# Opening of an attention and soft-MoE kernel: a load on another queue, two operations on another engine, and banks of two pools

## The chip, the cores and the metric

One core of one Trainium2 chip runs the kernel. The metric is the device time of one execution in microseconds (us). The kernel before took 471.74 us, the median of three runs (471.3 to 471.97).

## The reference

Two stages follow each other. The first is an attention over B = 4 batches and H = 8 heads (32 heads in all), with S = 768 rows of D = 64 columns, in which a query sees a key only if the two fall in the same bucket of a hash of six signs:

```python
q_bits = (np.einsum('bhsd,dk->bhsk', q, proj) > 0)
k_bits = (np.einsum('bhsd,dk->bhsk', k, proj) > 0)
mask = q_bucket[:, :, :, None] == k_bucket[:, :, None, :]
scores = scale * np.matmul(q, k.transpose(0, 1, 3, 2))
scores = np.where(mask, scores, -1000000000.0)
scores = scores - np.max(scores, axis=-1, keepdims=True)
attn = np.exp(scores)
attn = attn / (np.sum(attn, axis=-1, keepdims=True) + 1e-09)
return np.matmul(attn, v)
```

The second is a soft mixture of eight experts on the 3072 rows of 512 columns that the first leaves: softmaxes over the rows and over the 32 slots, and two matrix products per expert. The change lies in the first 10 us of the first stage.

## The kernel before

Everything is in float32 (or its rounded form for the matmuls), transposed so that the 64 columns of a head lie on partitions. Two heads share a tile. The 32 heads run one after the other, overlapped; the order of the work is written by hand: every step is a small function that `at` puts into `plan` with a due time from the tables ONCE (first occurrences) and STEADY (the rest). `plan` is sorted by these times and the functions are called in that order, so on each engine and each queue the order of instructions is the order of the due times. Those of the opening are negative, from -120 on.

A head needs two tiles, `Y` and `X`, which the scores multiply in two passes. `Y` holds the high part of q and of k (rows 0 to 63), the hash bits as rows of signs (from row 64) and, sent later, the negated maxima of the rows; `X` holds cross terms. Head 0 gets its parts by a short path written for the opening, the other heads by copies.

The steps around the change, in the order of the due times:
- Loads: `first` (projection and constants, line 278), then the four halves of q and k of heads 0 and 1 (`load_half`, line 257, L259), then head 2's q and k (`load`, L255) and v, all on SP's queue.
- `spin` (line 320, L323): matmuls on a tile of ones, whose results nobody reads; 7 at the start, 1 after nearly every matmul of head 0's maxima, 2 at three later places.
- `first_copy` (L429, ScalarE), `first_bits` (line 431, L435, PE): the hash projections of head 0 for k (x = 1) and q (x = 0), into two banks of pool `p_st`.
- `more_bits` (line 442): the projections of heads 0 and 1 from the full tiles (L411), copied by ScalarE (L447) into `pts[0]`; `bits_rest` (line 449) turns them into signs on GpSimd (L406 there) for head 1, tile `bt`.
- `first_over` (line 424, L406 on VectorE): the same for head 0, in five pieces, from PSUM straight into `Y`.
- `first_hi` (L440, ScalarE) the high parts; `split_lo` (L375, GpSimd) the low parts; `copy_ident` (L337, GpSimd) the identity for transposes.
- `smax` (line 463): the scores of a block of 128 rows for the maxima alone, a matmul (L474) and the maximum on VectorE (L477, L480). A bank takes 512 columns of them, so that a head has nine maxima; the banks are the two of pool `p_sm`.
- `shift`, `shift_rows` (L489 to L502): the maxima are joined, transposed on PE (L499), copied by ScalarE (L502) and sent as `mr` into a row of `Y` by SP.
- Copies between partitions by DMA (`move`, L379): `spread_y`, `spread_bits` (four copies of `bt`, head 1) and `spread_l`, `spread_x` for the later heads on SP's queue; for head 0 `spread_l` and `spread_x` go on ScalarE's queue. `first_x` (L403, ScalarE) fills the rest of head 0's `X`.
- `scores` (L515, PE): the true scores, followed by the exponential on ScalarE (L519), the sums on GpSimd (L526, L532) and the product with v (L544).

PSUM has eight banks here: two of `p_sm`, three of `p_st`, one of `p_av` (spins and the product with v) and two of `p_mi`.

Of the kernel before, what the change touches and what calls it, by code (L numbers as in the profile page):

```python
# [9 lines left out]
F32 = mybir.dt.float32  # L10
# [80 lines left out]
    ('copy_ident',): -79.0, ('first_bits', 0): -117.0, ('first_bits', 1): -119.0, ('first_copy', 0): -116.0,  # L91
    ('first_copy', 1): -118.0, ('first_hi', 0): -107.0, ('first_hi', 1): -108.0, ('first_mz',): -96.0,
    ('first_over', 0, 0, 256): -110.0, ('first_over', 0, 256, 512): -100.0, ('first_over', 0, 512, 768): -99.0,
    ('first_over', 1, 0, 512): -111.0, ('first_over', 1, 512, 768): -109.0, ('first_rows', 0): -115.0,
# [95 lines left out]
def lsh_attention_soft_moe(  # L190
# [66 lines left out]
    def load_half(a):  # L257
        for x in (1, 0):
            nc.sync.dma_start(out=raw[D * a:D * a + D, x], in_=qk[x, 0, D * a:D * a + D])  # L259

# [4 lines left out]


    ones = cp.tile([P, 32], F32, name="ones")
    nc.vector.memset(ones, 1.0)
    XYs = [held.tile([P, 2, 2, S], F32R, name=f"XY{i}") for i, held in enumerate((yp, xp, yq))]
    Xs, Ys = [[t[:, :, n] for t in XYs] for n in range(2)]  # L270
    idle = Xs[2][:, 0, 0:P + 512]
    nc.vector.memset(idle.bitcast(F32), 1.0)
    eps = cp.tile([P, 1], F32, name="eps")
# [45 lines left out]

    def spin(n, cols=512):  # L320
        pt = p_av.tile([P, 512], F32, name="av")
        for _ in range(n):
            nc.tensor.matmul(pt[:, 0:cols], idle[:, 0:P], idle[:, P:P + cols], start=True, stop=True)  # L323

    spin(7)


# [77 lines left out]
    def over(out, pt, rows, eng=nc.vector, cols=slice(0, HC)):  # L405
        eng.tensor_scalar(out=out, in0=pt[rows, cols], scalar1=con[rows, C_TH:C_TH + 1],  # L406
                          scalar2=con[rows, C_AM:C_AM + 1], op0=ALU.is_gt, op1=ALU.mult)
# [16 lines left out]
    def first_over(x, a, b):  # L424
        j = 2 * x + a // 512
        over(Ys[0][64:80, x, a:b], first_pt[x], slice(32 * j, 32 * j + 16), cols=slice(a % 512, a % 512 + b - a))

# [35 lines left out]
    def smax(h, t, part):  # L463
        s = st[h]
        if "mx" not in s:
            s["mx"] = mp.tile([P, NT, 2], F32, name="mx", bufs=2)
        mx = s["mx"].rearrange("p t a -> p (t a)")
        n = 2 * t + part
        key = "sm", n // 4, (n % 4 + 1) // 2
        if key not in s:  # L470
            s[key] = p_sm.tile([P, 512], F32, name="smx")
        pt = s[key]
        o, a, b = ((0, 0, 512), (0, 512, S), (256, 0, 256), (0, 256, S))[n % 4]
        nc.tensor.matmul(pt[:, o:o + b - a], Ys[h % N_Y][0:96, 0, t * P:(t + 1) * P], Ys[h % N_Y][0:96, 1, a:b],  # L474
                         start=True, stop=True)
        if n % 4 == 2:
            nc.vector.tensor_reduce(out=mx[:, n - 1:n + 1], in_=pt.rearrange("p (a x) -> p a x", a=2),  # L477
                                    axis=AX.X, op=ALU.max)
        elif n % 4 != 1:
            nc.vector.reduce_max(out=mx[:, n:n + 1], in_=pt, axis=AX.X)  # L480
        if h == 0 and t < NT - 1:
            spin(1)

# [381 lines left out]
    for n in (1, 0):  # L865
        at(first_copy, n)
        at(first_bits, n)
        at(first_hi, n)
    for xab in ((1, 0, 512), (0, 0, 256), (1, 512, S), (0, 256, 512), (0, 512, S)):
        at(first_over, *xab)  # L870
    at(more_bits)
    for n in range(3):
        at(spin, 2, tag=n)
    at(bits_rest)
# [264 lines left out]
```

## Time and profile before

| | |
|---|---|
| median of three runs | 471.74 us |
| the profiled execution | 471.47 us |
| its span, first to last instruction | 469.7 us |
| PE busy | 456.4 us (97%) |
| VectorE, ScalarE, GpSimd busy | 389.0, 247.4, 327.6 us |
| first DMA issue on SP | at 0.74 us |
| ScalarE's table load (L298) | at 0.74 us, 1.28 us long |

Times in the views are in us from the first instruction. PE is TensorE's matmuls, PEld its weight loads, DVE is VectorE, ACT ScalarE, POOL GpSimd. A queue's own instructions are those of SPq and ACTq: issuing a DMA takes the queue some time, and the data starts later. L with a number is the line of the kernel; since `over` and `move` are helpers, several steps share the lines L406 and L379, and are told apart by the tiles (`XY<-bt`, `XY<-stage`, `XY<-mr`).

### The profile page before, as it was taken

Reading aid. Unit: us, or ns where it says so; the run is one execution under the profiler, and the core shown is the slowest. Engines: PE = TensorE matmul, PEld = TensorE weight load, DVE = VectorE, ACT = ScalarE, POOL = GpSimd, SP = SyncE. Lnnn points to the kernel's source line nnn. Section 1 sums busy time; section 2 is a strip of 40 time slices with the busy share of each in tenths; the row PEclk is TensorE's granted clock in tenths of the full one; section 3 lists DMA queues with packets and bytes.
Section 4 is the critical chain, followed back from the end, with each engine's and each line's share of the span. In section 5 each row is a group of like instructions: output and inputs, shape, how many; then the busy total and the mean of one; then the engine's idle time right before and its main releaser. Section 6 shows DMA issues by size and latency. Waiting matters only on the chain.

```text
span 469.7 us, 10655 instructions
## 1 busy us (share of the span) xinstructions
PE 456.4 (97%) x3980; PEld 287.8 (61%) x3980; DVE 389.0 (83%) x723; ACT 247.4 (53%) x462; POOL 327.6 (70%) x205
## 2 busy tenths in 40 slices
PE   7999999999999999999999999999999999999993
PEld 3565666666666666666656666666666666553472
DVE  7868898989798988889898989897979886787952
ACT  5364556464657555555556464646565545531242
POOL 7878778878775988787868987787759878810000
PEclk9999999999999999999999999999999999999998
DMA  5757677777774767878683878685846677899997
GB/s 159 200 139 165 162 170 230 163 238 164 218 172 150 170 194 165 238 167 241 145 235 106 205 203 202 206 202 159 200 135 166 177 180 258 297 387 409 408 365 305
DMA packets 39535, 99.29 MB, mean 211 GB/s; under 512 B 7326, under 2 KB 13612, under 8 KB 39484
## 3 DMA queue, kind: packets, MB, share of 16 engines
q1 hardware_dynamic: 39292, 98.16, 72.3%
q8 instruction: 31, 0.51, 0.4%
q10 hardware_dynamic: 160, 0.39, 0.4%
q14 instruction: 20, 0.16, 0.1%
q0 software_dynamic: 32, 0.07, 0.0%
HBM read 52.76 MB, written 6.29 MB: 126 GB/s over the span
## 4 chain that ended last, share of the span: by engine, by line
PE 91%; DVE 3%; DMA 2%; issue 1%; ACT 0%; SPq 0%; DVEq 0%; ACTq 0%
PE st L515 29%; PE av L544 25%; PE smx L474 16%; PE qs L1050 3%; PE qh L1000 3%; PE mi L556 2%; PE mi L411 2%; PE mi L607 2%; PE mi L572 2%; DMA XY<-mr 1%; PE mi L592 1%; DMA stage<-qk 1%; PE mi L762 1%; PE mi L499 1%; PE qh L1070 1%
## 5 line engine op out<-in xcount | busy, mean ns | idle before, releaser
L532 POOL TENSOR_TENSOR acc<-acc,pt 128x768 f32<-128x768 f32 x125 | 229.1, 1833 | 9.6
L519 ACT ACTIVATE pt<-st 128x512 f32<-128x512 f32 x288 | 164.3, 597 | 62.3 <-PE st L515 56.5
L515 PE MATMUL st<-XY 128*128 128x256 f32 (+1 forms) x768 | 178.0, 347 | 0.7 <-DMA XY<-mr 0.7
L480 DVE TENSOR_REDUCE mx<-smx 128x1 f32<-128x512 f32 x192 | 131.1, 688 | 24.9 <-PE smx L474 22.8
L515 PEld LDWEIGHTS st<-XY 128*128 128x128 f32 x768 | 125.0, 189 | 19.0 <-ACT pt L519 1.7
L544 PE MATMUL av<-pt,v 128*32 128x384 f32 x1536 | 133.1, 486 | 0.0
L474 PE MATMUL smx<-XY 96*128 96x512 f32 (+1 forms) x384 | 118.4, 357 | 1.2 <-DVE mx L477 0.9
L526 POOL TENSOR_TENSOR acc<-pt 128x768 f32<-128x768 f32 x32 | 58.9, 1839 | 53.1 <-ACT pt L519 53.1
L544 PEld LDWEIGHTS av<-pt,v 128*32 128x32 f32 x1536 | 49.7, 110 | 72.8 <-issue 71.6
L474 PEld LDWEIGHTS smx<-XY 96*128 96x128 f32 x384 | 66.0, 188 | 30.8 <-issue 9.6
L477 DVE TENSOR_REDUCE mx<-smx 128x2 f32<-128x512 f32 x96 | 65.8, 686 | 6.1 <-PE smx L474 5.5
L548 ACT COPY avs<-av 128x384 f32<-128x384 f32 x32 | 15.3, 477 | 82.9 <-PE av L544 82.8
L564 DVE RECIPROCAL dl<-sm 128x128 f32<-128x128 f32 x45 | 38.8, 915 | 13.9 <-ACT sm L559 10.1
L372 DVE TENSOR_REDUCE stage<-stage 128x768 fp32r<-128x1536 f32 x28 | 49.0, 1782 | 0.0
L365 ACT ACTIVATE stage<-stage 128x768 fp32r<-128x768 f32 x28 | 22.6, 836 | 5.3 <-DMA stage<-qk 3.8
L609 DVE TENSOR_TENSOR xq<-mi,r 128x256 f32<-128x256 f32 x45 | 17.4, 416 | 1.1 <-PE mi L607 1.1
L833 DVE STREAM_TRANSPOSE w<-call 32x256 f32<-32x256 f32 (+2 forms) x48 | 14.9, 333 | 1.7 <-PE qh L1000 1.1
L1050 PE MATMUL qs<-w 128*32 128x128 f32 (+1 forms) x352 | 15.3, 303 | 0.0
L607 PE MATMUL mi<-ident,avs 128*128 128x128 f32 x90 | 14.8, 272 | 0.0
L607 PEld LDWEIGHTS mi<-ident,avs 128*128 128x128 f32 x90 | 11.7, 140 | 4.0
L1050 PEld LDWEIGHTS qs<-w 128*32 128x32 f32 x352 | 10.6, 110 | 5.2 <-issue 2.2
L411 PE MATMUL mi<-stage,pb 128*32 128x384 f32 x120 | 12.8, 498 | 0.7 <-DMA stage<-qk 0.7
(183 smaller groups left out, 330.8 us busy)
## 6 DMA issues: line engine op xcount, KB each, us to landing
w<-w SPq DMA_DIRECT2D x53, 512.0 KB
XY<-stage SPq DMA_DIRECT2D x62, 384.0 KB
XY<-stage SPq DMA_DIRECT2D x62, 192.0 KB
stage<-qk SPq DMA_DIRECT2D x28, 384.0 KB
v<-vt SPq DMA_DIRECT2D x32, 192.0 KB
out<-stage SPq DMA_DIRECT2D x12, 512.0 KB
stage<-w SPq DMA_DIRECT2D x7, 512.0 KB
xq<-w SPq DMA_DIRECT2D x3, 512.0 KB
```

Source lines behind the costliest of these rows:

```text
L372: nc.vector.tensor_reduce(out=w[:, 2 * x + 1], in_=stage[:, x:n + 1:n - x].rearrange("p t s -> p s t"), axis=AX.X, op=ALU.add, negate=True)
L474: nc.tensor.matmul(pt[:, o:o + b - a], Ys[h % N_Y][0:96, 0, t * P:(t + 1) * P], Ys[h % N_Y][0:96, 1, a:b], start=True, stop=True)
L477: nc.vector.tensor_reduce(out=mx[:, n - 1:n + 1], in_=pt.rearrange("p (a x) -> p a x", a=2), axis=AX.X, op=ALU.max)
L480: nc.vector.reduce_max(out=mx[:, n:n + 1], in_=pt, axis=AX.X)
L515: nc.tensor.matmul(pt[:, o:o + b - a], x[:, 1, i * P:(i + 1) * P], x[:, 0, a:b], start=first, stop=not first)
L519: nc.scalar.activation(pts[i // 2][:, 512 * u:512 * u + 512], pt, AF.Exp, scale=D ** -0.5)
L526: nc.gpsimd.tensor_tensor(out=s["acc"], in0=pr[:, 0:S], in1=pr[:, S:2 * S], op=ALU.add)
L532: eng.tensor_tensor(out=s["acc"], in0=s["acc"], in1=pr[:, a * S:(a + 1) * S], op=ALU.add)
L544: nc.tensor.matmul(s["av"][D * c + d:D * c + d + 32, 0:HC], s["v"][:, i, d:d + 32], pr[:, o + c * HC:o + (c + 1) * HC], start=(i == 0), st ...
L564: nc.vector.reciprocal(out=st[h]["rs"][:, k * P:(k + 1) * P], in_=st[h]["sm"][:, k * P:(k + 1) * P])
L607: nc.tensor.transpose(pt[:, o:o + P], st[h + a]["avs"][:, k * P:(k + 1) * P], ident)
L1050: nc.tensor.matmul(po[32 * j:32 * j + 32], hTs[g][:, f, 32 * j:32 * j + 32], wt[1, x, 2 * g + f // 4, j].rearrange("p (f m) -> p f m", f=4 ...
```

## The change

One half of k goes on ScalarE's queue. The spins take 256 columns instead of 512 and are doubled in number, and the tile of ones that they read is smaller and is filled first. The pieces of `first_over` of q from column 256 on go to GpSimd, with due times before `bits_rest`; since they are read there from `pts[0]`, a new step `first_out` copies them out of PSUM on ScalarE. Of head 0's maxima every second bank is taken from `p_st`.

```diff
-    ('first_over', 0, 0, 256): -110.0, ('first_over', 0, 256, 512): -100.0, ('first_over', 0, 512, 768): -99.0,
+    ... ('first_out',): -110.5,
+    ('first_over', 0, 0, 256): -110.0, ('first_over', 0, 256, 512): -108.9, ('first_over', 0, 512, 768): -108.8,
...
     def load_half(a):
         for x in (1, 0):
-            nc.sync.dma_start(out=raw[D * a:D * a + D, x], in_=qk[x, 0, D * a:D * a + D])
+            eng = nc.scalar if x > a else nc.sync
+            eng.dma_start(out=raw[D * a:D * a + D, x], in_=qk[x, 0, D * a:D * a + D])
...
+    XYs = [held.tile([P, 2, 2, S], F32R, name=f"XY{i}") for i, held in enumerate((yp, xp, yq))]
+    Xs, Ys = [[t[:, :, n] for t in XYs] for n in range(2)]
+    idle = Xs[2][:, 0, 0:P + 256]
+    nc.vector.memset(idle.bitcast(F32), 1.0)
     ones = cp.tile([P, 32], F32, name="ones")
     nc.vector.memset(ones, 1.0)
-    XYs = [held.tile([P, 2, 2, S], F32R, name=f"XY{i}") for i, held in enumerate((yp, xp, yq))]
-    Xs, Ys = [[t[:, :, n] for t in XYs] for n in range(2)]
-    idle = Xs[2][:, 0, 0:P + 512]
-    nc.vector.memset(idle.bitcast(F32), 1.0)
...
-    def spin(n, cols=512):
+    def spin(n, cols=256):
...
-    spin(7)
+    spin(14)
...
     def first_over(x, a, b):
         j = 2 * x + a // 512
-        over(Ys[0][64:80, x, a:b], first_pt[x], slice(32 * j, 32 * j + 16), cols=slice(a % 512, a % 512 + b - a))
+        cols = slice(a % 512, a % 512 + b - a)
+        if x or a == 0:
+            over(Ys[0][64:80, x, a:b], first_pt[x], slice(32 * j, 32 * j + 16), cols=cols)
+        else:
+            over(Ys[0][64:80, x, a:b], pts[0][:, 512:1024], slice(32 * j, 32 * j + 16), nc.gpsimd, cols)
+
+    def first_out():
+        for a in (256, 512):
+            rows, cols = slice(32 * (a // 512), 32 * (a // 512) + 16), slice(a % 512, a % 512 + 256)
+            nc.scalar.copy(pts[0][rows, 512:1024][:, cols], first_pt[0][rows, cols])
...
         if key not in s:
-            s[key] = p_sm.tile([P, 512], F32, name="smx")
+            pool = p_st if h == 0 and (key[1] + key[2]) % 2 else p_sm
+            s[key] = pool.tile([P, 512], F32, name=names[pool])
...
         if h == 0 and t < NT - 1:
-            spin(1)
+            spin(2)
...
+    at(first_out)
     for xab in ((1, 0, 512), (0, 0, 256), (1, 512, S), (0, 256, 512), (0, 512, S)):
         at(first_over, *xab)
     at(more_bits)
     for n in range(3):
-        at(spin, 2, tag=n)
+        at(spin, 4, tag=n)
```

## Rows read from the trace of the kernel before

**Rows 1.** The page, the chain that ended last: share of the span by engine

```profile
PE 91%; DVE 3%; DMA 2%; issue 1%; ACT 0%; SPq 0%; DVEq 0%; ACTq 0%
```

**Rows 2.** Timeline of PE: start, length, engine, line, operation, count, idle before

```profile
20.20 0.50 PE L474 MATMUL smx<-XY 96*128 96x512 f32 x1 [0.19 <-DVE mx L477]
20.71 0.74 PE L515 MATMUL st<-XY 128*128 128x256 f32 x4
```

**Rows 3.** Waits from 12 to 27 us: who for whom, total, times, longest

```profile
PEld st L515 <- DMA XY<-mr: 0.3, 1, 0.3
```

**Rows 4.** Timeline of SP's queue, 8 to 20.8 us (the issuing instructions)

```profile
10.30 0.71 SPq L379 DMA_DIRECT2D XY<-stage  x1
11.05 0.59 SPq L283 DMA_DIRECT2D pt<-cst  x1
11.74 3.70 SPq L379 DMA_DIRECT2D XY<-bt  x4
15.54 1.50 SPq L379 DMA_DIRECT2D XY<-stage  x2
18.04 0.82 SPq L379 DMA_DIRECT2D XY<-mr  x1
```

**Rows 5.** DMA queues, 14 to 16.7 (q10, ScalarE's), 16.7 to 19.9 (q1, SP's): packets, MB, share

```profile
q10 hardware_dynamic: 156, 0.39, 68.9%
...
q1 hardware_dynamic: 256, 0.60, 81.5%
```

**Rows 6.** Timeline of SP's queue, 0 to 8 us: the four halves

```profile
1.18 2.49 SPq L259 DMA_DIRECT2D stage<-qk  x4
```

**Rows 7.** Timeline of PE at 7.4 us: the matmuls of `more_bits`

```profile
7.41 0.85 PE L411 MATMUL mi<-stage,pb 128*32 128x384 f32 x8 [0.66 <-DMA stage<-qk]
```

**Rows 8.** Timelines of VectorE and of PE, the maxima of head 0

```profile
9.46 1.09 DVE L406 TENSOR_SCALAR XY<-st,con 16x256 fp32r<-16x256 f32 x2
...
15.90 0.69 DVE L480 TENSOR_REDUCE mx<-smx 128x1 f32<-128x512 f32 x1 [0.22 <-PE smx L474]
...
11.32 0.50 PE L474 MATMUL smx<-XY 96*128 96x512 f32 x1 [0.72 <-DVE mx L477]
...
15.46 0.40 PE L474 MATMUL smx<-XY 96*128 96x512 f32 x1
```

**Rows 9.** Timeline of ScalarE, 8 to 20.8 us (ACTq: its DMA issues)

```profile
8.33 0.48 ACT L447 COPY pt<-mi 128x384 f32<-128x384 f32 x1 [2.10 <-PE mi L411]
8.70 1.57 ACT L440 CAST stage<-stage 128x768 fp32r<-128x768 f32 x2
...
12.65 2.07 ACTq L379 DMA_DIRECT2D XY<-stage  x2
14.76 1.57 ACT L403 CAST XY<-stage 64x768 fp32r<-64x768 f32 x2 [3.01 <-POOL ident L337]
17.76 0.26 ACT L502 CAST mr<-mi 12x128 fp32r<-12x128 f32 x1 [1.43 <-PE mi L499]
```

**Rows 10.** Timeline of GpSimd, 8 to 20.8 us

```profile
9.01 1.66 POOL L406 TENSOR_SCALAR bt<-pt,con 128x384 fp32r<-128x384 f32 x1 [2.08 <-ACT pt L447]
...
10.80 3.62 POOL L375 TENSOR_TENSOR stage<-stage 128x768 fp32r<-128x768 f32 x2
14.38 0.29 POOL L337 CAST ident<-pt 128x128 fp32r<-128x128 f32 x1
```

**Rows 11.** Groups of GpSimd by shape, whole span: count | busy us, mean ns | idle

```profile
L344 POOL MEMSET XY<- 1x1536 f32 x2 | 2.7, 1374 | 0.1
L343 POOL MEMSET XY<- 32x1536 f32 x2 | 2.7, 1372 | 0.3 <-POOLq L1130 0.3
...
L406 POOL TENSOR_SCALAR bt<-pt,con 128x384 fp32r<-128x384 f32 x1 | 1.7, 1658 | 2.1 <-ACT pt L447 2.1
```

**Rows 12.** Stretches: PE, PEld, DVE, ACT, POOL busy (count), PE clock, DMA share, GB/s

```profile
10.00:11.00 1.00, 0.60 (x3) 0.19 (x1) 0.96 (x2) 1.00 (x3) 1.00 (x3) 1.00 0.00 0
11.00:12.00 1.00, 0.68 (x3) 0.38 (x3) 1.00 (x3) 0.75 (x2) 1.00 (x1) 1.00 0.36 83
```

More of the change, by code (lines that the diff above doesn't have):

```diff
@@ L91 @@
     ('copy_ident',): -79.0, ('first_bits', 0): -117.0, ('first_bits', 1): -119.0, ('first_copy', 0): -116.0,
-    ('first_copy', 1): -118.0, ('first_hi', 0): -107.0, ('first_hi', 1): -108.0, ('first_mz',): -96.0,
-    ('first_over', 0, 0, 256): -110.0, ('first_over', 0, 256, 512): -100.0, ('first_over', 0, 512, 768): -99.0,
+    ('first_copy', 1): -118.0, ('first_hi', 0): -107.0, ('first_hi', 1): -108.0, ('first_mz',): -96.0, ('first_out',): -110.5,
+    ('first_over', 0, 0, 256): -110.0, ('first_over', 0, 256, 512): -108.9, ('first_over', 0, 512, 768): -108.8,
     ('first_over', 1, 0, 512): -111.0, ('first_over', 1, 512, 768): -109.0, ('first_rows', 0): -115.0,
```

## The prediction, made before the changed kernel ran

> **What bounds the kernel now.** I read four views: the chain of the whole span, the waits around the first scores, the timelines of each queue and engine over the first 21 us, and the DMA engines' share by stretch. The chain is 91% TensorE [rows 1], and from the first scores (`scores`, L515) on the matmuls follow each other without a gap that matters. So a change in the opening is worth what it moves the start of that stream, 20.71 us [rows 2], and nothing else.
>
> What released that start? The waits say a DMA: `XY<-mr`, the row of negated maxima that `shift_rows(0)` sends; PE waited 0.3 us for it [rows 3], the last matmul before it having begun at 20.20 [rows 2]. The maxima themselves are not what made it late. SP issued the row at 18.04 [rows 4], 2.67 before it was used. In SP's queue it stood behind the two `XY<-stage` copies issued from 15.54 on (`spread_y(2)`, 384 KB, and `spread_l(1)`, 192 KB). Between 16.7 and 19.9 the SP queue moved 0.60 MB, exactly those two, in 81.5% of the 16 engines' time; before that, from 14 to 16.7, ACT's queue moved 0.39 MB, `spread_l(0)` and `spread_x(0)`, in 68.9% [rows 5]. So the start of the stream hangs on DMA work that lies end to end from 14 to 20 us, and the change must be judged by what it does to that.
>
> **The k half on ScalarE.** The condition `x > a` moves one of four halves, k of the first head; the other three go out one issue earlier, 2.49/4 = 0.62 us [rows 6]. The last half releases `more_bits` at 7.41 [rows 7]. The gain there lies between nothing (engines already full) and 0.62. The first data can start as much earlier as ScalarE issues before SP's 1.18, at the time of SP's first issue (0.74 in the table), which is 0.44; I take 0.45. If ScalarE's table load (1.28 us, in the table) goes first, it is nearer zero.
>
> **Spins and memset order.** The spin operand is 384 columns instead of 640 and is cleared first, and 14 matmuls of 256 columns replace 7 of 512: the same columns, starting a little sooner. I cost them at nothing: PE stands idle for 0.66 us after them and the first bits, until the last half lands [rows 7]. That is the cover; without it they would cost what they take beyond it. The later spins lie among the maxima of head 0, which the sum doesn't rest on.
>
> **The two additions of bits.** On VectorE the two operations of 16x256 took 1.09 us at 9.46 [rows 8], between two maxima. PE meanwhile had both banks full: its fifth matmul of the maxima waited until 11.32, and the last of the eight from there began at 15.46, 0.59 apart [rows 8]. With the operations gone and five banks in rotation instead of two, the fifth can start once GpSimd has delivered its columns, at 10.0 by the times below, and the last maximum, which begins at 15.90, near 14.6: a gain of about 1.3.
>
> What replaces them: ScalarE copies two 16x256 pieces out of PSUM (`first_out`), and GpSimd does the two operations. In program order the copies stand behind `more_bits`' own copy (L447), which in before starts at 8.33 and lets the next instruction start 0.37 later [rows 9]. With the 0.45 that is 7.88; 256 columns scale to 0.25 apart and 0.36 long, so the first piece is ready at 8.61 and `first_hi` starts at 8.75, against 8.70. GpSimd begins 0.2 after ScalarE's end (8.81 to 9.01 [rows 9, 10]): 8.8.
>
> The price of 16x256 on GpSimd is not in the trace. The nearest row is the same operation on 128x384, 1658 ns [rows 11]. Fewer partitions buy nothing: one partition and 32 of the same 1536 columns cost 1374 and 1372. By columns it is 1658 x 256/384 = 1105; a fixed part would add a little, and I take 1.15, since this row is the only one of the same operation. Below, the pace of the two subtractions on 128x768 (3.62 us [rows 10]) gives 1.81 x 256/768 = 0.60; above, the whole 1658. With 1.15 the two end at 9.95 and 11.1, and `bits_rest`, queued behind them, at 12.75 instead of 10.67: 2.1 late. GpSimd's idle time before 9.01 (2.08 us [rows 10]) doesn't cover this, because the copies come behind `more_bits`.
>
> **What is queued behind.** Everything GpSimd does next comes 2.1 later: `split_lo(0, .)` at 10.80, `copy_ident` at 14.38 [rows 10].
> - SP: the four `XY<-bt` copies began at 11.74, when SP had been free since 11.64, while bits were ready at 10.67 [rows 4, 10]: 1.07 of cover. Ready at 12.75, they start at 12.8 and take 3.70 again, so `spread_y(2)` goes out at 16.5 at the latest, against 15.54.
> - ScalarE: `spread_l(0)` waits for the first `split_lo`, 12.65 before [rows 9], 14.75 now; `spread_x(0)` follows, then the two `first_x`, which waited for GpSimd already (3.01 us idle at 14.76). Two issues at 0.62 to 0.82 each [rows 4, 6] and 1.57 for the `first_x` end between 17.55 and 17.95, and the copy of the maxima row, 17.76 before [rows 9], starts about where it did. The 1.3 won on VectorE ends here, in ScalarE's order; `copy_ident`, now done at 16.8, would hold the transpose back too.
> - DMA: a copy issued at 10.30 shows no share in 10 to 11 and 0.36 in 11 to 12 [rows 12], so data starts some 1.3 us after issue. ACT's pair starts at 16.05 instead of 14.0, when the engines have little else. Then the pair (68.9% of 2.7 = 1.86 us) and SP's two (81.5% of 3.2 = 2.6 us) stand in the same stretch: 4.46 us if packed without a gap, 5.9 if with the gaps of before. From 16.05 that is 20.5 to 21.95, against 19.9: the row comes 0.6 to 2.05 late. I take 1.2, a little under the middle, because two queues together leave fewer gaps than one.
>
> **The sum.** +1.2 us at the first scores, between +0.6 and +2.05 by the packing alone, and down to +0.2 with the cheapest operation. PE stands still meanwhile, and nothing later on PE has slack to give it back. The profiled execution took 471.47, span 469.7; the median of the three is 471.74, 0.27 more, so the difference is put on the median: 471.74 + 1.2 = 472.9.
>
> **Rivals.**
> 1. *GpSimd is cheaper, and the delay is covered.* If most of the 1658 is paid once, or columns are cheap, two operations take 0.6 each: `bits_rest` ends at 11.65, just when SP is free, `spread_l(0)` goes out 1.0 late (13.65), and ACT's pair, 1.86 us of the engines from 14.95, ends at 16.8, where data of `spread_y(2)` starts (15.54 + 1.3). +0.2 for what doesn't pack: 471.9. For it: only one instruction of this kind is in the trace, so its fixed part is unknown. Against it: 4.3 ns a column is in one measured row, and 2.4 ns for the subtractions beside it. The Trainium skill, page "GPSIMD Engine Reference", section 3.1, has a tight loop at about 1.8 cycles an element, at that page's 1.2 GHz an estimate of 0.38 us for 256 columns, which would make this rival true. By that rule 1658 ns would be 5.2 cycles an element: the trace does not agree with it.
> 2. *Faster: the maxima decide.* If ACT's pair and SP's two copies pass through the engines beside each other rather than in turn, and GpSimd is cheap, then the row leaves as soon as the maxima are there. The maxima end 1.3 sooner; it decides once the two operations take under 0.4 each, so that `bits_rest` ends by 11.25. Up to -1.2: 470.5. Against it: the share is 0.69 to 0.82 with one queue alone [rows 5], so there is little room beside, and the copies of `bt` can't go out before SP is free at 11.64.
> 3. *Slower still.* The 1658 is fixed whatever the size: two cost 1.0 more, and all behind them: 473.9. The same comes of the halves not landing sooner (+0.45) with a little of each.
> 4. *It doesn't do what it says.* One k half moves, not two; that is in the sum.
>
> **How the numbers follow.** Forecast 0.50 (472.9, own range 472.2 to 473.5), first rival 0.28 (471.9), faster 0.10 (470.5), slower still 0.12 (473.9). The range leaves the whole of the second rival and the far end of the third out: 471.0 to 474.2. About 0.2% (0.94 us) is what a measurement can tell: 472.7 is the border. Of the forecast some 0.36 of its 0.50 lies above it, with all of the third rival 0.48; below 470.8 the second rival and a little of the first's tail, 0.12; within, 0.40.
>
> **What would show it.** Right: GpSimd's two 16x256 operations at 1.1 to 1.2 us from about 8.8, `bits_rest` to about 12.75, ACT's DMA at about 14.75, PE waiting over 1 us for `XY<-mr` at about 21.9, while the last maximum of head 0 begins near 14.6. Wrong: operations of 0.6 or less, `more_bits` before 6.5 or not moved at all, scores beginning by 20.7, or a PE wait before the scores for VectorE rather than the row. The forecast also falls if scores begin late and the end of the kernel doesn't, which would mean that PE's stream had slack. A longer pause on PE could also lower the granted clock; it is 1.00 in the stretches of rows 12, where PE paused 0.72 us [rows 8].

## The result, and the profile after

| | before | after |
|---|---|---|
| median | 471.30 us (9 runs) | 474.07 us (472.42 to 477.91) |
| the profiled execution | 471.47 us | 474.89 us |
| its span | 469.7 us | 473.1 us |
| first matmul of the true scores | 20.71 | 22.96 |

One of nine executions of the changed kernel took 574.4 us at a mean granted clock of 0.757 and is neither in the range above nor in the ratio.

The ratio of after to before is 1.0062 (95%: 1.0039 to 1.0085): slower by about 2.9 us, where +1.2 was forecast. The sign was right, the size was not. The chain that ended last is TensorE's as before [rows 1]:

```profile
PE 91%; DVE 3%; DMA 2%; issue 1%; POOL 1%; SPq 0%; ACT 0%; DVEq 0%; POOLq 0%
```

So the place to look is again the start of the stream of scores. Timeline of PE of the changed kernel (start, length, engine, line, operation, count, idle before), which answers [rows 2, 7, 8]:

```profile
6.65 0.85 PE L412 MATMUL mi<-stage,pb 128*32 128x384 f32 x8 [0.67 <-DMA stage<-qk]
9.31 0.79 PE L485 MATMUL smx<-XY 96*128 96x512 f32 x1 [1.81 <-DVE XY L407]
10.33 0.41 PE L485 MATMUL st<-XY 96*128 96x256 f32 x1
11.18 0.41 PE L485 MATMUL st<-XY 96*128 96x256 f32 x1
...
17.85 0.40 PE L485 MATMUL smx<-XY 96*128 96x512 f32 x1
...
22.96 0.63 PE L526 MATMUL st<-XY 128*128 128x256 f32 x4
```

`more_bits` comes 0.76 earlier than in [rows 7]. Then PE stands for 1.81 us ahead of the first maximum, where before it stood for nothing, and the next matmuls of the maxima come 0.85 apart (10.33 to 11.18). The reason for the pause is in VectorE's timeline, against [rows 8]:

```profile
8.72 1.12 DVE L407 TENSOR_SCALAR XY<-st,con 16x256 fp32r<-16x256 f32 x2 [1.96 <-ACT pt L436]
...
18.29 0.69 DVE L491 TENSOR_REDUCE mx<-smx 128x1 f32<-128x512 f32 x1 [0.22 <-PE smx L485]
```

VectorE's second addition, q's columns 0 to 256, waits 1.96 us for L436: `first_out` on ScalarE. All of them read the bank of `first_pt[0]`, the addition and the first copy in the same 16 partitions, the second copy 32 partitions further on, and VectorE begins only behind both copies (below, they end at 8.68). ScalarE's timeline, against [rows 9], shows why that is late:

```profile
7.57 0.48 ACT L457 COPY pt<-mi 128x384 f32<-128x384 f32 x1 [1.86 <-PE mi L412]
7.94 0.74 ACT L436 COPY pt<-st 16x256 f32<-16x256 f32 x2
...
14.68 1.60 ACTq L380 DMA_DIRECT2D XY<-stage  x2
...
20.14 0.25 ACT L513 CAST mr<-mi 12x128 fp32r<-12x128 f32 x1 [2.26 <-PE mi L510]
```

`first_out` stands behind the copy L457, which waits for `more_bits`, which waits for the last half to land. So VectorE hangs on a load that it did not need before. PE's first maximum stood behind `more_bits` before too, but now ScalarE's three copies and VectorE's addition lie between the two. The Trainium skill, page "PSUM — Partial Sum Buffer", section "PSUM bank collisions raise a hardware error", says that two engines must not touch one bank in the same 32 partitions at once, two readers included, and that a dependency has to keep them apart. The trace agrees in so far as the readers do run one after the other; by that rule only the first copy had to be kept apart from the addition, and no run here let VectorE start beside either.

The pause has a second effect. Stretches of the changed kernel (busy time and count of PE, PEld, DVE, ACT, POOL; then the granted clock, DMA share, GB/s):

```profile
8.00:10.00 2.00, 0.69 (x2) 0.59 (x3) 1.09 (x2) 1.95 (x5) 1.50 (x2) 0.61 0.19 72
10.00:12.00 2.00, 2.00 (x9) 1.72 (x8) 1.06 (x2) 1.75 (x3) 1.90 (x2) 0.50 0.18 41
...
14.00:16.00 2.00, 2.00 (x10) 1.72 (x9) 1.14 (x3) 0.00 (x0) 2.00 (x2) 0.69 0.10 25
```

The granted clock is at 0.50 (1.2 GHz) for most of 8 to 16 us, where it was 1.00 before from 10 to 12 [rows 12]. It fell during the 1.81 us in which PE had nothing to do, and it makes PE the bound of the maxima: VectorE now waits for PE at most of them. The last maximum begins at 18.29, not at 15.90 [rows 8] or at the 14.6 of the forecast.

The other side of the forecast is in the timelines of GpSimd and of SP's queue, against [rows 10] and [rows 4], and in the DMA queues from 16 to 18.5 (q10, ScalarE's) and from 18 to 21 us (q1, SP's), against [rows 5]:

```profile
8.41 2.54 POOL L407 TENSOR_SCALAR XY<-pt,con 16x256 fp32r<-16x256 f32 x2 [1.48 <-ACT pt L436]
11.04 1.65 POOL L407 TENSOR_SCALAR bt<-pt,con 128x384 fp32r<-128x384 f32 x1
```

```profile
12.72 3.33 SPq L380 DMA_DIRECT2D XY<-bt  x4
...
20.43 0.82 SPq L380 DMA_DIRECT2D XY<-mr  x1
```

```profile
q10 hardware_dynamic: 160, 0.39, 71.4%
...
q1 hardware_dynamic: 219, 0.59, 85.7%
```

These came as forecast: `bits_rest` ends at 12.69 (forecast 12.75), ScalarE's pair is issued at 14.68 (14.75), its 0.39 MB move from 16 us on (16.05), SP's 0.59 MB end at 21. What did not come as forecast is the row itself: it is issued at 20.43, 2.39 later than in [rows 4], since the maxima are late. So in this kernel two things are late, the transfers and the maxima. In this execution the maxima are the later: the transfers are done at 21, the engines stand almost still until the row moves at 21.87, and PE does not wait for the row at 22.96. The stretch between, in the same order as above:

```profile
21.00:21.80 0.80, 0.72 (x5) 0.34 (x3) 0.80 (x2) 0.00 (x0) 0.42 (x1) 1.00 0.01 4
```

What each of the two would cost without the other, this profile can't say.

### The profile page after: what moved, and what is told of

Same layout as the page of the kernel before. It is cut to its first block, busy times and chain, and to the rows that moved or that the text cites. A ratio compares the mean times of both kernels' runs of the same rounds, so it can differ in the third digit from the quotient of the medians.

```text
span 473.1 us, 10702 instructions
## 1 busy us (share of the span) xinstructions
PE 457.9 (97%) x4003; PEld 292.2 (62%) x4003; DVE 388.0 (82%) x721; ACT 247.2 (52%) x464; POOL 329.8 (70%) x207
## 4 chain that ended last, share of the span: by engine, by line
PE 91%; DVE 3%; DMA 2%; issue 1%; POOL 1%; SPq 0%; ACT 0%; DVEq 0%; POOLq 0%
PE st L526 27%; PE av L555 26%; PE smx L485 16%; PE qs L1062 3%; PE qh L1012 3%; PE mi L412 3%; PE mi L567 2%; PE mi L618 2%; PE mi L583 2%; PE av L324 1%; PE mi L603 1%; PE mi L773 1%; DMA stage<-qk 1%; PE mi L510 1%; PE qh L1082 1%
## 5 line engine op out<-in xcount | busy, mean ns | idle before, releaser
L491 DVE TENSOR_REDUCE mx<-smx 128x1 f32<-128x512 f32 x190 | 129.7, 688 | 27.0 <-PE smx L485 24.3
L485 PE MATMUL smx<-XY 96*128 96x256 f32 (+1 forms) x378 | 117.0, 359 | 3.3 <-DVE XY L407 1.8
L488 DVE TENSOR_REDUCE mx<-smx 128x2 f32<-128x512 f32 x94 | 64.4, 685 | 5.3 <-PE smx L485 4.6
```

## The experiments

All times are medians; each ratio is to the kernel before, run beside it on the same chip (medians from 471.53 to 471.81 us). A kernel's profile is one execution. Two reasons were to be told apart: the forecast's (GpSimd's load delays the transfers ahead of the row) and the one that the profile after suggests (VectorE's wait for the copies, and the clock that falls in PE's pause).

| label | kernel | first scores at | median us | ratio (95%) |
|---|---|---|---|---|
| e1_out_early | after, copies of `first_out` early | 22.71 | 475.20 | 1.0073 (1.0046 to 1.0100) |
| e2_out_late | after, copies late | 22.30 | 474.79 | 1.0074 (1.0057 to 1.0090) |
| e3_over_back | after, additions back on VectorE | 20.96 | 473.22 | 1.0033 (1.0010 to 1.0055) |
| e4_spin_fill | after, spins in the pause | 23.77 | 475.23 | 1.0081 (1.0057 to 1.0105) |
| e5_k_half | before + k half | 20.24 | 470.71 | 0.9989 (0.9967 to 1.0010) |
| e6_spins | before + spins | 20.40 | 472.65 | 1.0014 (0.9995 to 1.0032) |
| e7_banks | before + banks | 20.55 | 472.01 | 1.0017 (0.9998 to 1.0036) |
| e8_pool_only | before + GpSimd's part | 23.27 | 473.23 | 1.0033 (1.0016 to 1.0051) |
| e9_pool_load | before + GpSimd's load alone | 23.01 | 473.71 | 1.0052 (1.0036 to 1.0069) |
| e10_wait_only | before + VectorE's wait alone | 23.69 | 473.98 | 1.0052 (1.0034 to 1.0070) |
| e11_wait_fill | the same with PE's pause filled | 22.21 | 474.18 | 1.0052 (1.0028 to 1.0075) |
| e12_half_banks | before + k half + banks | 20.19 | 471.16 | 0.9994 (0.9974 to 1.0013) |
| e13_rest_first | after, `bits_rest` first, copies late | 22.52 | 475.23 | 1.0070 (1.0046 to 1.0095) |
| e14_load_after | before + load behind `bits_rest` | 22.04 | 473.91 | 1.0042 (1.0023 to 1.0062) |

### The four parts one at a time

**e5_k_half.**

```diff
+            eng = nc.scalar if x > a else nc.sync
+            eng.dma_start(out=raw[D * a:D * a + D, x], in_=qk[x, 0, D * a:D * a + D])
```

> The kernel before with one part of the change: the second halves of k load on ScalarE's queue, everything else as before. The forecast's reason: more_bits starts 0.45 to 0.8 us earlier than 7.41, the maxima 0.5 earlier or as before, the row of maxima is bound by the same transfers, so 470.8 to 472.2 us, no difference from before (471.6). Rival (the transfer on a second queue shares the engines with the q halves and the first bits land no earlier, or TensorE's opening gets an extra pause): 472.8 to 473.6, which would be all that the change without GpSimd's part lost (473.2).

Timeline of PE of this kernel:

```profile
6.51 0.85 PE L412 MATMUL mi<-stage,pb 128*32 128x384 f32 x8 [0.24 <-DMA stage<-qk]
...
20.24 0.64 PE L516 MATMUL st<-XY 128*128 128x256 f32 x4
```

`more_bits` comes 0.90 earlier, the scores 0.47 earlier than in [rows 2]. The median is 1.0 us under that of before, but the interval holds 1. The expectation speaks of second halves; the edit moves one half, k of the first head. Its 0.90 is that of one execution: over all kernels here `more_bits` begins between 7.07 and 7.41 without the half and between 6.51 and 7.91 with it, about 0.3 earlier by the medians, so the size of the gain is not settled. PE doesn't wait for the row at 20.24.

**e6_spins.**

```diff
+    idle = Xs[2][:, 0, 0:P + 256]
...
+    def spin(n, cols=256):
...
+    spin(14)
```

> The kernel before with one part of the change: the filling matmuls have 256 columns and are twice as many, and their operand is filled before the column of ones. The forecast's reason: same columns, nothing lost, 470.8 to 472.2 us with the first maxima at 8.19 us and the last at 15.90 as in the trace of before. Rival (the clock's state in the opening follows the filling matmuls): TensorE's granted clock reaches full speed at another time than 6.0 us of before's trace, and the time comes to 472.8 to 473.6, all that the change without GpSimd's part lost.

No difference that the interval shows: 1.0014 (0.9995 to 1.0032), first scores at 20.40. Nothing, or up to 1.5 us, stays open; the profile gives no reason for a loss.

**e7_banks.**

```diff
+            pool = p_st if h == 0 and (key[1] + key[2]) % 2 else p_sm
+            s[key] = pool.tile([P, 512], F32, name=names[pool])
```

> The kernel before with one part of the change: half of the first head's maxima take banks of the pool st. The forecast's reason: VectorE binds the maxima as before or less (last maximum of head 0 between 15.0 and 15.9 us), the row is bound by the transfers in front of it, so 470.6 to 472.2 us. Rival (the first scores, which take banks of the same pool, wait for the maxima that hold them): scores start 1 to 2 us later than 20.71 and 472.6 to 473.6.

The last maximum begins at 15.07 (before 15.90), the scores at 20.55 (before 20.71), the time doesn't change. Earlier maxima alone buy nothing that shows. In this execution the clock was at 0.50 from 19.95 us to 23.36, at the start of the scores, though none of PE's pauses from 14 us to there was longer than 0.41.

**e8_pool_only.**

```diff
+    ('first_over', 0, 256, 512): -108.9, ('first_over', 0, 512, 768): -108.8, ('first_out',): -110.5,
...
+            over(Ys[0][64:80, x, a:b], pts[0][:, 512:1024], slice(32 * j, 32 * j + 16), nc.gpsimd, cols)
...
+    at(first_out)
```

> The kernel before with one part of the change: the two additions of bits of q's columns 256 to 768 on GpSimd, with the copies of first_out ahead of them on ScalarE, everything else as before. more_bits stays at 7.41, so the copies come at 8.3 to 8.7, VectorE's second addition waits for them as it did after the whole change (until 9.4 to 9.6 us), bits_rest ends near 13.4 (before 10.67), spread_y(2) comes past 16.7 on SyncE's queue. Theory 1 (the forecast's transfers alone): the first scores wait for a row that lands 1.5 to 2.3 us later, 473.0 to 474.0. Theory 2 (besides that, the pause of 1.8 us ahead of the first maximum lets TensorE's granted clock fall to 0.5): the maxima come in steps of 0.85 us, the last at 18.5 or later, 474.0 to 475.5. If neither holds and the other parts of the change are the cost: 471.2 to 472.4.

PE's pause of 1.81 us and the steps of 0.85 us come back with this part alone; the last maximum begins at 18.64, and PE does not wait for the row at the scores (23.27). The ratio is 1.0033, 1.5 us, at the low end of what the transfers alone should have cost, and under the 474.0 that the clock was to add. It is the only single part with a loss that its interval shows. The four ratios sum to 1.0053, the whole change has 1.0062.

### GpSimd's load and VectorE's wait, each by itself

**e9_pool_load.** Two additions that nobody reads, ahead of `bits_rest`.

```diff
     def bits_rest():
+        for _ in range(2):
+            over(pts[0][0:16, 512:768], pts[0], slice(0, 16), nc.gpsimd, slice(0, 256))
         over(st[0]["bt"], pts[0], slice(0, P), nc.gpsimd)
```

> The kernel before, with two additions of bits of 16 x 256 on GpSimd ahead of bits_rest that nobody reads (they read pt and write a free place of it); VectorE keeps its own work, the maxima don't change. It measures GpSimd's load alone: bits_rest ends 2.5 us later (near 13.2 against 10.67), spread_y(2) is issued past 16.5, the maxima stay where they are (last at 15.9). If the transfers' delay is what the change cost (theory 1): the first scores wait for the row until 22 to 22.5 and 472.9 to 473.6 us. If the wait of VectorE and the clock are the cost (theory 2): within 0.15% of before, 471.0 to 472.4.

Timelines of VectorE and of PE:

```profile
17.28 0.69 DVE L482 TENSOR_REDUCE mx<-smx 128x1 f32<-128x512 f32 x1 [0.23 <-PE smx L476]
...
23.01 0.74 PE L517 MATMUL st<-XY 128*128 128x256 f32 x4 [0.77 <-DMA XY<-mr]
```

VectorE waits for no copy here, and PE has no pause ahead of the maxima, yet the time is 2.2 us above before's. GpSimd's load costs time by itself: the reason of the forecast holds. How it costs it, this profile doesn't show cleanly. The granted clock rose to 1.00 only at 13.51 us in this execution, against 6.04 in before; `more_bits` ran at half speed, 1.51 instead of 0.85 us, the last maximum began at 17.28 instead of 15.90 [rows 8], and the row was issued 1.37 later than in [rows 4]. So the scores' 2.3 us are in part those of late maxima. The same load with the maxima on time is in e14 below.

**e10_wait_only.** The copies on ScalarE, read by nobody; all additions on VectorE.

```diff
+    ('first_out',): -110.5,
...
+            nc.scalar.copy(pts[0][rows, 512:1024][:, cols], first_pt[0][rows, cols])
```

> The kernel before, with the two copies of first_out on ScalarE at the change's place, and all additions of bits on VectorE as before: the copies are read by nobody. It measures the wait of VectorE alone: its second addition waits until about 9.1 us, TensorE pauses 1.8 us ahead of the first maximum (near 9.7), the granted clock falls to 0.5, the last maximum comes at 18.5 to 19; bits_rest stays near 10.7. Theory 2: the row leaves near 21 and 473.2 to 474.5 us. Theory 1: the row is bound by the transfers, which are not delayed, so 471.2 to 472.4.

Timelines of VectorE, of PE and of SP's queue, and below them a stretch:

```profile
9.29 1.12 DVE L406 TENSOR_SCALAR XY<-st,con 16x256 fp32r<-16x256 f32 x2 [1.82 <-ACT pt L431]
...
9.88 0.79 PE L479 MATMUL smx<-XY 96*128 96x512 f32 x1 [1.80 <-DVE XY L406]
...
18.61 0.40 PE L479 MATMUL smx<-XY 96*128 96x512 f32 x1
...
23.69 0.64 PE L520 MATMUL st<-XY 128*128 128x256 f32 x4
...
21.19 0.81 SPq L379 DMA_DIRECT2D XY<-mr  x1
```

```profile
10.00:12.00 2.00, 2.00 (x5) 1.21 (x5) 1.65 (x4) 2.00 (x4) 1.71 (x3) 0.50 0.00 0
```

Without any load on GpSimd the wait of VectorE, the pause of PE and the clock at 0.50 come, the row leaves at 21.19, 3.15 after [rows 4], and the time is 2.4 us above before's. The wait that the forecast didn't see costs as much by itself as GpSimd's load does. The edit brings a little more than the wait: the two copies also put ScalarE's `first_hi` 0.58 later than in [rows 9] (9.28), and SP's last pair of copies goes out 0.64 later than in [rows 4] (16.18). The maxima, with the last matmul at 18.61, are later by far more (15.46 in [rows 8]).

**e11_wait_fill.** The same, and eight spins of 512 columns in PE's pause.

```diff
+    at(spin, 8, tag="w")
     at(bits_rest)
```

> The kernel before with first_out's copies (VectorE waits as in the run with the wait alone), and eight filling matmuls of 512 columns between more_bits and the first maximum, so that TensorE has no pause there. If it is the clock that the wait costs: maxima in steps of 0.56 us, the last near 17.2, the row leaves 1.3 us later than before's 18.04 and the time is 0.5 to 1.0 us under that of the run with the wait alone. If the clock costs nothing and the order of the work everything: the same time as with the wait alone.

Timeline of PE:

```profile
9.90 0.42 PE L479 MATMUL smx<-XY 96*128 96x512 f32 x1
10.46 0.33 PE L479 MATMUL smx<-XY 96*128 96x256 f32 x1
...
17.14 0.40 PE L479 MATMUL smx<-XY 96*128 96x512 f32 x1
...
22.21 0.63 PE L520 MATMUL st<-XY 128*128 128x256 f32 x4
```

The profile does what the clock's part asked for: the first maximum at the same time (9.90, with the wait alone 9.88), steps of 0.56 instead of 0.85 us, the last matmul 1.47 earlier, the scores 1.48 earlier. The times don't follow: 474.18 against 473.98, with runs from 472.07 to 476.31. So 1.5 us is what the clock takes from the maxima in a profile, and that it is a part of the lost time is not shown. Filling this pause did not keep the clock up in every execution either: seven of the twelve had a mean granted clock of 0.994 or more and a median of 473.15 us, the other five a lower one and a median of 475.08.

### Mending the change

**e1_out_early**, `('first_out',): -110.5` to `-112.5`, ahead of `more_bits`' copy.

> The changed kernel with one due time altered: first_out at -112.5 instead of -110.5, so that ScalarE's two copies out of PSUM stand ahead of the copy of more_bits. Theory A (VectorE's second over, q's columns 0 to 256, waits for the copies because both read one bank, 1.96 us idle in the changed kernel, and PE and its clock follow): the copies end near 6.7, VectorE starts that over by 6.8 instead of 8.72, the first maximum's matmul starts near 7.6 instead of 9.31, the granted clock stays 1.00, GpSimd ends bits_rest near 11.2, inside the 1.07 us of cover on SP, and the scores begin at 20.7 or sooner: 470.3 to 471.5 beside 471.3 of before. Theory B (the loss is the DMA work behind GpSimd, as forecast): bits_rest is early here too, so also about 471.3 to 471.8. Theory C (the banks, the spins or the load on ScalarE's queue cost it): about 474 as in the changed kernel.

Timeline of PE:

```profile
7.91 1.23 PE L412 MATMUL mi<-stage,pb 128*32 128x384 f32 x8 [2.05 <-DMA stage<-qk]
9.06 0.79 PE L485 MATMUL smx<-XY 96*128 96x512 f32 x1
```

VectorE's wait is gone (its three additions ran from 5.87 to 7.83), but in this execution the last half landed 1.26 us later than in the profile after, PE paused for 2.05 us in front of `more_bits` instead, and the clock fell as before. The expected gain didn't come; as PE's order puts `more_bits` ahead of the first maximum, the pause moves to the load. As 1.26 of the 2.05 are that late landing, this execution can't say whether the clock would have fallen without it.

**e2_out_late**, `-110.5` to `-109.5`, behind VectorE's own additions.

> The changed kernel with first_out at -109.5 instead of -110.5, behind VectorE's over of columns 0 to 256: VectorE no longer waits for ScalarE's copies, while GpSimd's two operations start as late as in the changed kernel (8.4) and everything behind them on GpSimd stays 2 us late. Theory A (VectorE's wait and the clock behind it): the first maximum near 8, the last begins near 14.6 to 15, and what is left is the forecast's DMA term, the row of maxima landing 0.6 to 2 us later than in before: 472.0 to 473.0. Theory B (the DMA work behind GpSimd is the whole loss): nothing is won, 474. Theory C (banks, spins, load): 474.

Timelines of VectorE and PE, and below them a stretch:

```profile
14.53 0.69 DVE L491 TENSOR_REDUCE mx<-smx 128x1 f32<-128x512 f32 x1 [0.23 <-PE smx L485]
...
18.44 1.10 PE L485 MATMUL smx<-XY 96*128 96x512 f32 x2 [1.19 <-DMA XY<-bt]
...
22.30 1.22 PE L526 MATMUL st<-XY 128*128 128x256 f32 x4
```

```profile
20.00:22.00 2.00, 1.68 (x6) 1.07 (x5) 1.58 (x3) 0.00 (x0) 1.89 (x3) 0.50 0.84 174
```

This is the kernel that the forecast described: no wait, the last maximum at 14.53 (forecast 14.6), and then everything waits for GpSimd and the transfers. The scores begin 1.59 late (forecast 1.2). And it is no faster than the whole change: PE, 0.33 us busy between 16 and 18, has its pauses there, the last of them for copies of `bt` and not for the row, the clock is at 0.50 from 18.53 to 25.36, and four matmuls of the scores take 1.22 us instead of 0.74. Taking the unforeseen wait away wins nothing.

**e4_spin_fill**, `at(spin, 15, tag="w")` between `more_bits` and the first maximum.

> The changed kernel with 15 more idle matmuls of 256 columns on PE between more_bits and the first maximum, which fill the wait from 7.5 to 9.31 and take nothing of it away. Theory A1 (the clock that fell in the wait makes most of the loss): granted clock 1.00 throughout, matmuls of the maxima 0.56 to 0.6 apart instead of 0.85, the last maximum begins near 16 instead of 18.29, then the row of maxima waits for the DMA work behind GpSimd, and the scores begin near 22: 472.4 to 473. Theory A2 (the wait alone costs it, the clock is without effect): 474, and the last maximum still near 18.

The maxima kept full speed (last one at 16.45), and then PE waited 2.03 us for the row and began the scores at 23.77. The pause moved again. How much of the 2.03 is chance is open: eleven of the row's twelve packets began by 21.35 in this execution, and the last at 22.52. The clock was at 0.50 here from 21.25 to 28.08, over the start of the scores.

**e3_over_back.** The additions back on VectorE, no `first_out`; the other three parts stay.

```diff
-    ('first_over', 0, 256, 512): -108.9, ('first_over', 0, 512, 768): -108.8,
+    ('first_over', 0, 256, 512): -100.0, ('first_over', 0, 512, 768): -99.0,
...
-    at(first_out)
```

> The changed kernel without first_out and with the two operations of bits back on VectorE at their old due times; the k half on ScalarE's queue, the spins and the banks of two pools stay. Theory A: no wait of VectorE for ScalarE, clock at 1.00, more_bits at 6.65 as in the changed kernel, the last maximum begins 0.7 to 1.5 us before the 15.90 of before, and the scores begin at 20.0 to 20.7: 470.5 to 471.3. Theory B: GpSimd's work as early as or earlier than in before, 470.5 to 471.3 as well. Theory C (banks, spins, load): 473 to 474.

First scores at 20.96, 1.0033 (1.0010 to 1.0055). About half of the loss goes with GpSimd's part. The other half is more than the single runs of the three remaining parts explain (their ratios sum to 1.0020), though within their intervals; its cause stays open. In this execution, too, the clock rose late, at 10.56 us, and `more_bits` took 1.51 us, so 20.96 is not the edit's alone.

**e12_half_banks.** e5 and e7 together.

> The kernel before with two parts of the change: the second halves of k on ScalarE's queue and the banks of two pools for the first maxima. GpSimd and the filling matmuls as before. If the transfers bind the first row (more_bits is what starts them): the gain of the k half alone, 470.3 to 471.1 us, the first scores at 20.2 as in that run although the last maximum comes before 15. If the maxima bind: scores at 19.7 or earlier, 469.8 to 470.5. If the banks cost of themselves: 471.4 to 472.4.

Timeline of PE, and below it a stretch:

```profile
20.19 1.22 PE L517 MATMUL st<-XY 128*128 128x256 f32 x4 [0.16 <-DMA XY<-mr]
```

```profile
20.00:22.00 2.00, 1.84 (x9) 1.81 (x9) 0.81 (x2) 0.55 (x1) 1.52 (x2) 0.50 0.89 352
```

The last maximum begins at 14.95, 0.65 earlier than with the k half alone, and the scores at the same time (20.19 and 20.24): PE waits 0.16 us for the row here, and not at all in e5. So with the maxima this early the transfers bind, as the forecast read them. The first four matmuls of the scores take 1.22 us at a clock of 0.50, against 0.64 in e5, and PE's pauses before it were 0.21 us or less from 14 us on. Neither ratio differs from 1.

### Which of GpSimd's products holds the row

**e14_load_after.** The unread additions behind `bits_rest`.

```diff
         over(st[0]["bt"], pts[0], slice(0, P), nc.gpsimd)
+        for _ in range(2):
+            over(pts[0][0:16, 512:768], pts[0], slice(0, 16), nc.gpsimd, slice(0, 256))
```

> The kernel before with the same two unread additions on GpSimd as in the run with GpSimd's load alone, but behind bits_rest. The bits' transfers stay at 11.74 on SyncE's queue, split_lo starts 2.5 us later (13.3) and ends near 16.9, so spread_y(2) and spread_l(1) are issued at 15.5 to 17 against 15.54 and 16.3. If bits_rest's place costs (SyncE's queue is blocked behind the bits): 471.4 to 472.4 us, at least 1.3 us under the run with the load in front (473.7). If the split halves bind: 473.0 to 474.2 as there.

Timelines of SP's queue and of PE; the DMA queues from 17.2 to 18.9 us and from 19 to 20.5 us; and a stretch:

```profile
11.45 3.71 SPq L379 DMA_DIRECT2D XY<-bt  x4
15.27 1.50 SPq L379 DMA_DIRECT2D XY<-stage  x2
18.01 1.10 SPq L379 DMA_DIRECT2D XY<-mr  x1
...
22.04 0.77 PE L517 MATMUL st<-XY 128*128 128x256 f32 x4 [1.64 <-DMA XY<-mr]
```

```profile
q1 hardware_dynamic: 108, 0.33, 98.5%
q10 hardware_dynamic: 13, 0.00, 0.4%
...
q10 hardware_dynamic: 75, 0.20, 69.0%
q1 hardware_dynamic: 49, 0.10, 26.4%
```

```profile
24.00:26.00 2.00, 2.00 (x7) 1.63 (x7) 0.86 (x2) 1.19 (x2) 0.00 (x0) 0.50 0.35 88
```

SP's queue is on time throughout: the bits at 11.45, the copies at 15.27, the row at 18.01, all within 0.3 of [rows 4]. Still PE waits 1.64 us for the row, and the time is that of e9. So it isn't the bits' place in SP's queue; it is `split_lo`, which GpSimd begins at 13.00, 2.2 later than in [rows 10], and whose halves ScalarE can send only at 14.85. These then move one after the other with SP's copies: ScalarE's second copy, issued by 16.2, has almost no share from 17.2 to 18.9 and moves behind SP's first. The engines are busy for 98.9% and 95.4% of the two stretches, against 68.9% and 81.5% in [rows 5], and all four copies take from about 16 to 21 us: nearer to the 4.46 of the forecast's close packing than to its 5.9. The scores are 1.33 late, which is what was forecast for the whole change (1.2); the kernel is 2.1 late. Soon after its pause PE runs the scores at a clock of 0.50.

What that clock costs here can be read from ScalarE's timeline, where nine exponentials follow the scores of head 0; first before, then this kernel:

```profile
21.49 5.09 ACT L519 ACTIVATE pt<-st 128x512 f32<-128x512 f32 x8 [3.48 <-PE st L515]
26.80 0.60 ACT L519 ACTIVATE pt<-st 128x512 f32<-128x512 f32 x1
```

```profile
22.84 0.60 ACT L521 ACTIVATE pt<-st 128x512 f32<-128x512 f32 x1 [4.86 <-PE st L517]
...
29.67 0.60 ACT L521 ACTIVATE pt<-st 128x512 f32<-128x512 f32 x1
```

From the first start to the ninth it is 5.31 us in before, as in e5, e8 and e10, which run this stretch at full clock, and 6.83 here, with PE busy throughout from 24 to 26. So the delay of this execution is 1.33 us at the first scores, 2.87 at the last exponential of head 0 and 3.4 at the end of the span (469.7 and 473.1). In e2 the nine take 6.17.

**e13_rest_first.** The change with `('bits_rest',): -108.95` and `('first_out',): -109.5`.

> The whole change with two orders altered: bits_rest goes ahead of the two additions on GpSimd, and first_out comes after VectorE's own additions, so that VectorE doesn't wait for it. If the row was late by bits_rest's place and by VectorE's wait: bits_rest ends near 9.7, the bits' four transfers are issued near 11 as before (11.74), the maxima wait about 1 us for q's columns 256 to 512 and the last comes near 15.6, the first scores at 20.2 to 21: 470.8 to 472.2 us. If it is the halves that GpSimd splits behind these additions (split_lo still begins 2.5 us late, near 12.4) that hold the row: scores at 22 or later and 473.0 to 474.5.

The scores begin at 22.52, as in the second case of its expectation, but the time of 475.23 us is above that case's. A new wait is in PE's timeline, for GpSimd's addition:

```profile
12.01 0.50 PE L485 MATMUL st<-XY 96*128 96x512 f32 x1 [1.40 <-POOL XY L407]
```

The clock was at 0.50 there from 12.44 to 15.85 us. `split_lo` begins at 13.61. GpSimd's two additions stand ahead of it in either order, and the orders tried here don't mend the change.

## Why the prediction was right and wrong

- **What bounds the kernel**: right. The stream's start decides, and the transfers ahead of the row set it: e7 and e12 end the maxima earlier and start the scores no earlier than the transfers let them. Less right is that nothing later has slack: in the profile of before PE waits 0.70 us for a later row at 43.85 us, a wait that e6, e14 and after do not have.
- **The k half**: sign right, 0.45 at `more_bits` forecast, 0.76 measured in after and 0.90 in e5, both above the 0.62 that the forecast took for the most; by the medians over all kernels it is about 0.3, with single executions far apart. It may be worth 1 us by itself, which isn't shown (0.9989, 0.9967 to 1.0010).
- **Spins**: costed at nothing; e6 is not told apart from that.
- **GpSimd's price**: 1.15 forecast, 2.54/2 = 1.27 measured; `bits_rest` ended within 0.1 of the forecast, by luck: the additions began 0.4 sooner and took 0.24 more. The first rival (0.6) is out, and so is the third (1.66 each), although its 473.9 is near the result.
- **What is queued behind**: right at each issue (SP's bits, ScalarE's pair, the start of its data), wrong at the copy of the maxima row, 17.76 forecast and 20.14 measured.
- **The two additions on VectorE**: this step failed. It gave the maxima a gain of 1.3 (last at 14.6), and they came 2.39 late. It followed `first_out` on ScalarE up to GpSimd, which reads what it writes, and did not ask who else reads the bank that it reads. VectorE does, and waits. Its own signs tell the two apart: a PE wait of over 1 us for the row is not in the profile after, and a PE wait for VectorE, one of the signs of being wrong, is. e10 shows that this wait alone costs 2.4 us, and e2 that without it the last maximum is at 14.53: the gain was real, and the transfers hide it.
- **The row's delay**: +1.2 taken from 0.6 to 2.05. In the kernels with GpSimd's load and without VectorE's wait it is 1.59 (e2) and 1.33 (e14): the size was nearly right. Only e14 shows PE waiting for the row itself with the maxima on time, and there the packing that the forecast assumed is seen. In after it is 2.25, since the maxima are late too.
- **From the row's delay to the time**: the sum took one for one, and this failed as well. A delay of 1.33 at the scores stands beside 2.1 us of time (e14), 1.59 beside 3.2 (e2); in both the clock was at 0.50 over part of the first scores, which adds 1.5 us to head 0's exponentials in e14's profile and 0.9 in e2's. The last sentence of the prediction named the clock and gave it no price. The other way occurs too: 2.98 beside 2.4 (e10), with full speed at the scores. These are single profiles beside medians, and the clock is not the bulk of the loss: in the executions with a mean granted clock of 0.996 or more e8's four took 473.08 to 475.46 us, e9's two 472.58 and 473.13, e10's one 472.84 and e14's one 472.83, where such executions of before have medians of 471.0 to 471.5.
- **The second rival** needed a cheap GpSimd and two queues passing beside each other; GpSimd was not cheap, and in e14 the copies of the two queues moved one after the other.

The forecast of +1.2 thus named one of two causes, either of which is enough: GpSimd's load (e9, e14) and VectorE's wait (e10) each cost 2.1 to 2.4 us, and together, in e8 and in after, no more than 1.5 and 2.9. They don't add, since the scores wait for the later of the two. What stays open is in how many executions the clock falls and what that adds to each median, and where e3's 1.7 us come from. No version here beats the kernel before by more than its interval; e5 comes nearest.

## What to carry to other kernels

When a copy is moved to another engine, list who else reads the bank that it reads, and not only who reads what it writes: the other reader inherits every wait of the copy. A late release of TensorE's stream is priced with the clock behind it, not one for one, and taking away one of two equally late causes shows no gain, so load and wait are best tried each by itself on the kernel before.

## What the runs showed of the hardware

- The granted clock fell to 0.50 (1.2 GHz) in a pause of TensorE of 1.81 us in after, and stayed there until about 15 us; in the kernel before there was no fall by a pause of 0.72 [rows 8, 12]. But it also fell in e7 and e12, where no pause from 14 us on was longer than 0.41 and 0.21, so these runs give no length of pause from which on it falls. The Trainium skill, page "TensorE: Matmul & The Clock Gate", part 1, names these two speeds, the lower as that of an engine that has been idle; the matmul of 96x512 agrees, at 0.79 us (9.31 in after) and 0.40 (17.85).
- GpSimd's addition took 1.27 us on 16x256 and 1.65 on 128x384: from these two, an estimate of about 3 ns a column and 0.5 us fixed.
- Copies on two queues moved in the order of their issue, each nearly alone (98.5% against 0.4% in e14), and they kept the engines busy for 98.9% and 95.4% of two stretches, where the kernel before had 68.9% and 81.5% [rows 5].
